# A one-column gelu behind each block's last output tile, and the mask of one attention unit moved to TensorE

## The chip, the cores and the metric

The kernel runs on one core of a Trainium2 chip. Times are microseconds (us) on the device. The time before is 360.91 us, the median of three runs (360.09 to 361.98); the profiled execution took 361.28 us, and its span, the part that the trace covers, is 359.4 us.

## What is computed

Two things in a row: windowed attention over 8 batches with 8 heads each, then a gated feed-forward block on the result. Cut to what matters:

```python
# attention: q, k, v are (8, 8, 576, 64) float32
rel = pos[:, None] - pos[None, :]
mask_plain = (rel >= 0) & (rel < 32)                        # heads 0 to 3
mask_dil   = (rel >= 0) & (rel < 128) & (rel % 4 == 0)      # heads 4 to 7
scores = where(mask, q @ k.T / 8, -1e9)
x = softmax(scores) @ v              # put together to (4608, 512)

# feed-forward: w_gate and w_val are (512, 1536), w_out is (1536, 512)
g = x @ w_gate
out = (gelu(g) * (x @ w_val)) @ w_out
```

## The kernel before

**Units and blocks.** Two heads of one batch make a unit: 32 units, four for each batch, two "plain" and two "dilated". The 4608 tokens are cut into 9 blocks of 512. A block `c` is first multiplied with the gate and value weights (`ffn1`, 12 steps `nb`), then with the output weights (`ffn2`, four tiles `tb` of 128 tokens, 12 matmuls each). The attention of later units is woven into that work. Its schedule is written by hand: the order of the program text is the order of the instructions on each engine.

```python
def geglu(nb, banks):
    g = ffn.tile([P, CH], F16, tag="g")                     # a pool of three
    nc.scalar.activation(g, ps[:, banks[0], :], AF.Gelu)                          # L584, ACT
    nc.vector.scalar_tensor_tensor(u_all[:, nb, :], g, USCALE,
                                   ps[:, banks[1], :], ALU.mult, ALU.mult)        # L585, DVE
```

Each step of `ffn1` fills one PSUM bank with gate sums (weights `wg`) and one with value sums (`wv`), four matmuls each on line 562. There are two pairs of banks, so step `nb` writes into the banks of step `nb - 2`: the gate bank is free once ScalarE's gelu has read it, the value bank once VectorE's multiplication has.

Where the block before it ended with attention work that the new block still waits for (a flag `late`: blocks 2, 3 and 4), the first two steps are interleaved: all matmuls of steps 0 and 1 that have their inputs come first, the rest follow, and only then come the two `geglu`:

```python
def ffn1_two(c, pairs, order, split):
    kcs = parts_of(order)
    for group in [kcs[:-1], kcs[-1:]] if split else [[kc] for kc in kcs]:
        for nb in range(2):
            for gi in range(2):
                ffn1_part(c, nb, gi, pairs[nb][gi], group)
    for nb in range(2):
        geglu(nb, pairs[nb])
```

The output tile is read out of PSUM by ScalarE and stored:

```python
def store(c, tb, bank, eng):
    osb = osbp.tile([P, DM], F32, tag="osb")
    if eng == "act":
        nc.scalar.activation(osb, ps[:, bank, :], AF.Copy, bias=0.0, scale=1.0 / USCALE)   # L602
```

**Scores of a unit.** `emit_s` computes the scores on TensorE, takes the exponential on ScalarE, and masks in one of two ways. Either VectorE multiplies the exponentials with a mask of zeros and ones, or (`pe_mask`) TensorE first writes a bias of 0 or -60000 into the four banks, by a matmul with the identity, and adds the scores to it:

```python
def emit_s(n, b0, pe_mask=False):
    ...
    else:                                                   # a dilated unit; DW is 288
        if pe_mask:
            for i in range(4):
                mm(ps[:, b0 + i, 0:DW], ident, bias_d, start=True, stop=False, ...)   # L359
        ...                                                 # 12 small matmuls, L373
        pt = prb.tile([P, 4, DW], F16, tag="P", name=f"P{n}")
        nc.scalar.activation(pt, ps[:, b0 : b0 + 4, 0:DW], AF.Exp, bias=0.0, scale=scale)  # L375
    if pe_mask:
        return None
    def emit_mask():
        nc.vector.tensor_tensor(pt, pt, mb, ALU.mult)                                 # L383
    return emit_mask
```

**Values of a unit.** `emit_pv` multiplies the masked exponentials with ones and with the values (L455); VectorE then divides, in four steps: a transpose of the sums (L513), a reciprocal (L520), a transpose back (L522) and the product into `xT` (L537 for a dilated unit).

**The main loop.** A table says at which output tile and before which of its 12 matmuls each piece of attention is done: `v` the values of a unit and its reciprocals, `s` the scores of the next, `x` the product of the division, `m` the mask, `w` a unit's values with a division in two parts. The numbers are tile and matmul; 12 means after the tile's store.

```python
scores   = {0: range(4, 8), 1: range(8, 12), 2: range(12, 17), ...}
values_b = {1: range(8, 12), 2: range(12, 16), 3: range(17, 20), 4: range(22, 24), 5: range(27, 28)}
biased = (6, 7)
places = {
    1: "0.0m 1.3v 1.3s 1.3x 1.3m 2.5v 2.5s 2.5x 2.5m 3.0s 3.0m 3.6v 3.6x 3.12w",
    ...
}
for c in range(NCH):
    ...                              # ffn1, 12 steps of gelu; one emit_s behind them
        lone = c in values_b         # true for blocks 1 to 5
        for tb in range(4):
            ...
            ffn2(c, tb, bank, hooks)
            store(c, tb, bank, "dve" if c > 5 and tb == 3 else "act")
            ...
        late = lone and len(values_b[c]) > 2
```

In block 1 the scores of unit 8 come behind the last gelu, and those of unit 9 before matmul 3 of tile 1, behind the values of unit 8. Unit 9 is the second unit of batch 2, and it is a dilated one.

Of the kernel before, what the change touches and what calls it, by code (L numbers as in the profile page):

```python
# [9 lines left out]
F16 = mybir.dt.float16  # L10
F32 = mybir.dt.float32
AF = mybir.ActivationFunctionType
# [26 lines left out]
def kernel(  # L39
# [10 lines left out]
    nc = tc.nc  # L50
# [3 lines left out]
    P = 128  # L54
# [3 lines left out]
    CH = 512  # L58
# [25 lines left out]
    ffn = ctx.enter_context(tc.tile_pool(name="ffn", bufs=3))  # L84
    osbp = ctx.enter_context(tc.tile_pool(name="osbp", bufs=4))

    ones = const.tile([P, CH], F16, tag="ones")
# [135 lines left out]
    def load_batch_plain(b):  # L223
        st = load_qk_plain(b)
        sv = new_v(b)
        v_plain(b, sv, nc.sync)
        return st, sv
# [5 lines left out]
    def load_batch_rest(b):  # L233
        st, sv = tiles["plain", b]
        qd, rd = load_qk_dil(b)
        qp = cast_qk_plain(b, st)
        load_v_dil(b)
        v_cast(b, sv)
        new_qt(b)
        qtp_, qtd_, _ = tiles["qT", b]  # L240
        dst = qtd_.rearrange("p t h m i -> p (t h m) i")
        nc.sync.dma_start_transpose(out=dst[:, :, 0:P], in_=qd.rearrange("p t h r d -> p (t h r d)"))
        nc.sync.dma_start_transpose(out=dst[:, :, P:NCL], in_=rd.rearrange("p t h r d -> p (t h r d)"))
        dst = qtp_.rearrange("p t h c -> p (t h) c")
        for kb in range(5):
            n = min(P, S - kb * P)
            nc.sync.dma_start_transpose(
                out=dst[:, :, kb * P : kb * P + n], in_=qp[0:n, kb].rearrange("p t h d -> p (t h d)")
            )
        last_keys(b, 0, HK, nc.gpsimd)  # L250
# [6 lines left out]
    def is_plain(n):  # L257
        return pair(n) < NHP // 2
# [221 lines left out]
    def norm_both_r(n, b0):  # L480
        dt = nrm.tile([P, 18, 32], F32, tag="dt", bufs=1)
        for hl in range(2):
            nc.vector.transpose(  # L483
                dt[64 * hl : 64 * hl + 64].rearrange("p b c -> p (b c)"), both_rows(1 - hl, b0, hl)
            )
        recip(n, dt)
# [80 lines left out]
    def ffn1(c, nb, banks):  # L567
        for gi in range(2):
            ffn1_part(c, nb, gi, banks[gi], parts_of(range(NKC)))
        geglu(nb, banks)  # L570
# [12 lines that stand above are left out]
        g = ffn.tile([P, CH], F16, tag="g")  # L583
        nc.scalar.activation(g, ps[:, banks[0], :], AF.Gelu)  # L584
        nc.vector.scalar_tensor_tensor(u_all[:, nb, :], g, USCALE, ps[:, banks[1], :], ALU.mult, ALU.mult)  # L585

    def ffn2(c, tb, bank, hooks=None):
        for fc in range(NNB):
            for hook in (hooks or {}).get(fc, ()):
                hook()  # L590
            nc.tensor.matmul(  # L591
                ps[:, bank, :],
                u_all[:, fc, tb * P : (tb + 1) * P],
                wo_t[fc // 4][:, fc % 4, :],
                start=(fc == 0),
                stop=(fc == NNB - 1),
            )
# [57 lines left out]
    def den(n, b0, wide=False):  # L655
        emit_pv(n, b0, ("den",), wide)
        norm_r(n, b0, wide)
# [49 lines left out]
    scores = {0: range(4, 8), 1: range(8, 12), 2: range(12, 17), 3: range(17, 22), 4: range(22, 27), 5: range(27, 32)}  # L707
    values_b = {1: range(8, 12), 2: range(12, 16), 3: range(17, 20), 4: range(22, 24), 5: range(27, 28)}
    values_a = {3: {4: 16}, 4: {2: 20, 6: 21}, 5: {1: 24, 4: 25, 7: 26}, 6: {1: 28, 4: 29, 7: 30, 10: 31}}
    biased = (6, 7)  # L710

# [10 lines left out]
    for c in range(NCH):  # L724
        if 1 <= c and c + 2 < B:
            tiles["plain", c + 2] = load_batch_plain(c + 2)
            load_batch_rest(c + 2)
        pv_at = values_a.get(c, {})
        s_list = list(scores.get(c, ()))
        if c < 2:  # L730
            pairs = ((2, 3), (0, 1))
        else:
            pairs = (ends, (mm0 + 1, mm0 + 2))
        SB = 4 - mm0

        masks = []
        pend = None
        for nb in range(NNB):
            if nb == 0 and c < 2:
                ffn1_two(c, ((4, 5), (6, 7)) if c == 0 else ((6, 7), (0, 1)), range(NKC), False)  # L740
            elif nb == 0 and late:
                ffn1_two(c, pairs, (2, 3, 0, 1) if c in (2, 3) else range(NKC), True)
            elif nb > 1 or not (c < 2 or late):
                ffn1(c, nb, pairs[nb % 2])
            if pend is not None:
                (norm_both_x if is_plain(pend) else norm_x)(pend, SB)
                pend = None
            if nb in pv_at:
                pend = pv_at[nb]
                if is_plain(pend):  # L750
                    emit_both(pend, SB)
                    norm_both_r(pend, SB)
                else:
                    emit_pv(pend, SB, wide=True)
                    norm_r(pend, SB, wide=True)
            if c == 0 and nb in (9, 10):
                t_plain(1, q61, nb - 9, 4 + 2 * (nb - 9), ("act", "dve"))
            if c == 0 and nb in (8, 11):
                rr = rd1.rearrange("p t h r d -> p t (h r d)")
                hp = nb // 11  # L760
                t_dil(1, hp, qd1, 4096 + 512 * hp, 5120 + 512 * hp, ("dve", "dve"))
                t_rest(1, hp, (rr[:, 0], rr[:, 1]), 6144 + P * hp)
            if nb == NNB - 1 and c > 0 and s_list:
                n = s_list.pop(0)
                masks.append(emit_s(n, SB, pe_mask=n in biased))

        def s_next():
            if s_list:
                n = s_list.pop(0)
                masks.append(emit_s(n, SB, pe_mask=n in biased))  # L770

        def mask_next():
            mask = masks.pop(0) if masks else None
            if mask is not None:
                mask()


        def md(n):
            mask_next()
            den(n, 0, wide=True)  # L780

        if c == 0:
            load_batch_rest(2)
            ffn2(c, 0, 0, {5: [s_next]})
            store(c, 0, 0, "act")
            ffn2(c, 1, 1, {4: [s_next], 8: [lambda: md(4)]})
            store(c, 1, 1, "act")
            s_next()
            ffn2(c, 2, 0, {4: [lambda: md(5)], 6: [s_next], 9: [lambda: md(6)]})
            store(c, 2, 0, "act")  # L790
            ffn2(c, 3, 1, {2: [lambda: md(7), lambda: num(4, 4)], 8: [lambda: num(5, 6)]})
            store(c, 3, 1, "act")
            num(6, 2)
            num(7, 4)
        else:
            todo = list(values_b.get(c, ()))
            lone = c in values_b

            ends = (3, 0) if c == 1 else ends
            going = []  # L800

            def do(kind, tb):
                if kind == "s":
                    s_next()
                elif kind == "m":
                    mask_next()
                elif kind == "x":
                    norm_x(*going.pop(0))
                elif kind == "v":
                    n, flip = todo.pop(0), ends[tb % 2] != mm0  # L810
                    bank = mm0 + 1 - flip
                    emit_pv(n, bank, flip=flip)
                    norm_r(n, bank, flip=flip)
                    going.append((n, bank, flip))
                else:
                    n = todo.pop(0)
                    emit_pv(n, SB)
                    norm_parts(n, SB, min(S, (c + 2) * CH - n // NHP * S))

            for tb in range(4):  # L820
                at = [(fc, kind) for t, fc, kind in places.get(c, ()) if t == tb]
                hooks = {}
                for fc, kind in at:
                    if fc < NNB:
                        hooks.setdefault(fc, []).append(lambda kind=kind, tb=tb: do(kind, tb))
                bank = ends[tb % 2] if lone else mm0 + tb
                ffn2(c, tb, bank, hooks)
                store(c, tb, bank, "dve" if c > 5 and tb == 3 else "act")
                for fc, kind in at:
                    if fc == NNB:  # L830
                        do(kind, tb)

            late = lone and len(values_b[c]) > 2
            if c == 3:
                mm0 = 4 - mm0
            if c == 3 or not lone:
                ends = (mm0, mm0 + 3)
            while masks:
                mask_next()
# [28 lines left out]
```

The softmax here doesn't subtract the row's maximum and nothing guards it: scores larger than these inputs give would overflow.

## Time and profile before

| | busy, us | share of the span |
|---|---|---|
| PE (TensorE matmul) | 338.7 | 94% |
| DVE (VectorE) | 204.4 | 57% |
| ACT (ScalarE) | 145.8 | 41% |
| POOL (GpSimd) | 78.4 | 22% |

How to read it: L584 is line 584 of the kernel before; "PEld" is TensorE's load of weights, which goes on beside its matmuls. In the timeline a row gives the start, the time from the start of its first to the end of its last instruction, the engine, the line, what is written and read, and how many there are; brackets tell how long the engine had been idle and what ended that. The busy time of matmuls overlaps in part, since they are pipelined: rows of 512-column matmuls start 0.216 us apart (four of them take 0.86 us from the first's start to the next group's), although one is listed with 0.38 us.

The table load is a row of its own, ACT_TABLE_LOAD, with 1283 ns each: 7 on line 584 (gelu), 4 on line 375 and 2 on line 353 (exponential), and one at the start of the program.

### The profile page before, as it was taken

What the parts mean: (1) busy time and instruction counts of PE and PEld (TensorE: products, weight loads), DVE (VectorE), ACT (ScalarE), POOL (GpSimd) and SP (SyncE); (2) the same over time, 40 slices, a digit from 0 to 9 for tenths busy, and PEclk for the clock granted to TensorE, in tenths of its full rate; (3) what the DMA queues carried; (4) which work ended last, traced back from release to release, by engine and by line L of the source; (5) the groups of instructions that cost most, each with busy time, mean ns of one, the idle gap of its engine ahead of it and who ended that gap; (6) DMA issues with size and microseconds to landing.
All of it is one profiled execution on the core that took longest, in us unless ns stands there. A gap on an engine that the chain in (4) does not pass through costs nothing.

```text
span 359.4 us, 5962 instructions
## 1 busy us (share of the span) xinstructions
PE 338.7 (94%) x2326; PEld 164.2 (46%) x2326; DVE 204.4 (57%) x314; ACT 145.8 (41%) x212; POOL 78.4 (22%) x110
## 2 busy tenths in 40 slices
PE   5889999999898999899989999999999999999995
PEld 2554454444443444344544444544454444444442
DVE  3595446744695448773768855894489514403320
ACT  1733255253444354435453357326633123313320
POOL 2580334630531350063004500140000000000000
PEclk9889999999999999999999999999999999999999
DMA  8999999999999997699149952793100020020002
GB/s 198 237 181 211 221 154 204 166 154 255 199 124 213 186 163 152 161 174 142 60 120 193 135 95 79 179 158 79 69 22 0 31 88 0 3 84 32 2 30 88
DMA packets 107292, 45.31 MB, mean 126 GB/s; under 512 B 83040, under 2 KB 102496, under 8 KB 107264
## 3 DMA queue, kind: packets, MB, share of 16 engines
q1 hardware_dynamic: 84272, 31.21, 39.8%
q0 software_dynamic: 21456, 12.01, 26.6%
q10 hardware_dynamic: 1536, 1.70, 2.1%
q8 instruction: 18, 0.29, 0.3%
q14 instruction: 10, 0.08, 0.1%
HBM read 40.13 MB, written 9.44 MB: 138 GB/s over the span
## 4 chain that ended last, share of the span: by engine, by line
PE 66%; DVE 13%; DMA 13%; issue 3%; POOL 2%; ACT 1%; ACTq 0%; SPq 0%; DVEq 0%; POOLq 0%
PE ps L562 40%; PE ps L591 20%; PE ps L455 4%; DMA xT<-in_k_dram 4%; DMA st<-in_k_dram 3%; DMA wv<-in_moe_w_val_dram 3%; DMA wo<-in_moe_w_out_dram 2%; DVE P L383 2%; DVE xT L537 2%; DVE rb L522 2%; DVE dt L513 2%; DVE dt L483 2%; DVE u_all L585 2%; DVE xT L493 1%; DMA sv<-in_v_dram 1%
## 5 line engine op out<-in xcount | busy, mean ns | idle before, releaser
L562 PE MATMUL ps<-xT,wg 128*128 128x512 f16 x432 | 114.0, 379 | 5.1 <-ACT g L584 4.1
L585 DVE SCALAR_TENSOR_TENSOR u_all<-g,ps 128x512 f16<-128x512 f16 x108 | 72.8, 684 | 80.1 <-PE ps L562 70.0
L562 PE MATMUL ps<-xT,wv 128*128 128x512 f16 x432 | 113.8, 379 | 0.3 <-ACT osb L602 0.3
L584 ACT ACTIVATE g<-ps 128x512 f16<-128x512 f32 x108 | 63.7, 597 | 116.8 <-PE ps L562 116.6
L591 PE MATMUL ps<-wo,u_all 128*128 128x512 f16 x432 | 100.3, 380 | 0.1
L562 PEld LDWEIGHTS <-wv 128*128 128x128 f16 x432 | 42.2, 98 | 52.7 <-issue 2.6
L562 PEld LDWEIGHTS <-wg 128*128 128x128 f16 x432 | 41.1, 98 | 52.5 <-issue 5.5
L591 PEld LDWEIGHTS <-u_all 128*128 128x128 f16 x432 | 39.4, 98 | 45.4 <-issue 0.6
L602 ACT ACTIVATE osb<-ps 128x512 f32<-128x512 f32 x33 | 19.7, 598 | 38.1 <-PE ps L591 36.6
L199 POOL CAST qp<-st 128x2048 f16<-128x2048 f32 x6 | 11.4, 1896 | 100.1 <-DMA sv<-in_v_dram 54.3
L513 DVE STREAM_TRANSPOSE dt<-ps 128x576 f32<-128x576 f32 x23 | 17.9, 780 | 14.5 <-PE ps L455 14.3
L522 DVE STREAM_TRANSPOSE rb<-rc 128x576 f32<-128x576 f32 (+4 forms) x34 | 25.3, 743 | 1.2
L375 ACT ACTIVATE P<-ps 128x1152 f16<-128x1152 f32 x16 | 18.1, 1131 | 16.9 <-PE ps L373 13.0
L353 ACT ACTIVATE P<-ps 128x960 f16<-128x960 f32 x16 | 15.5, 970 | 12.8 <-PE ps L343 12.8
L537 DVE TENSOR_TENSOR xT<-ps,rb 128x576 f16<-128x576 f32 x16 | 17.9, 1129 | 0.3
L604 DVE TENSOR_SCALAR osb<-ps 128x512 f32<-128x512 f32 x3 | 2.1, 692 | 27.8 <-PE ps L591 27.8
L455 PE MATMUL ps<-P,ones 128*64 128x96 f16 (+5 forms) x174 | 12.0, 253 | 5.0 <-DVE P L383 2.9
L383 DVE TENSOR_TENSOR P<-P,mask_d 128x1152 f16<-128x1152 f16 x12 | 9.6, 800 | 10.2 <-ACT P L375 10.2
L383 DVE TENSOR_TENSOR P<-P,mask_p 128x1344 f16<-128x1344 f16 x14 | 12.4, 891 | 5.0 <-ACT P L354 4.9
L455 PEld LDWEIGHTS <-ones 128*64 128x64 f16 x174 | 7.7, 112 | 14.9 <-issue 10.8
L584 ACT ACT_TABLE_LOAD x7 | 9.0, 1283 | 12.4 <-PE ps L562 12.3
L483 DVE STREAM_TRANSPOSE dt<-ps 64x576 f32<-64x576 f32 x14 | 10.9, 781 | 0.4
(81 smaller groups left out, 238.9 us busy)
## 6 DMA issues: line engine op xcount, KB each, us to landing
out_dram<-osb SPq DMA_DIRECT2D x36, 256.0 KB, 2.0
sv<-in_v_dram SPq DMA_DIRECT2D x40, 128.0 KB, 3.6
st<-in_q_dram SPq DMA_DIRECT2D x24, 128.0 KB, 3.6
st<-in_k_dram SPq DMA_DIRECT2D x24, 128.0 KB, 3.1
qd<-in_q_dram POOLq DMA_DIRECT2D x7, 256.0 KB, 5.3
qd<-in_k_dram POOLq DMA_DIRECT2D x7, 256.0 KB, 6.7
vd<-in_v_dram POOLq DMA_DIRECT2D x7, 256.0 KB, 6.8
wg<-in_moe_w_gate_dram POOLq DMA_DIRECT2D x3, 512.0 KB, 7.5
```

Of the source, the lines that this page charges most:

```text
L375: nc.scalar.activation(pt, ps[:, b0 : b0 + 4, 0:DW], AF.Exp, bias=0.0, scale=scale)
L383: nc.vector.tensor_tensor(pt, pt, mb, ALU.mult)
L455: nc.tensor.matmul(o, lhs, rhs, start=st, stop=True, skip_group_check=True)
L483: nc.vector.transpose(dt[64 * hl : 64 * hl + 64].rearrange("p b c -> p (b c)"), both_rows(1 - hl, b0, hl))
L513: nc.vector.transpose(dst, den)
L522: nc.vector.transpose(rb[:, 0 : 32 * nb].rearrange("p (b c) -> p b c", c=32), bass.AP(tensor=rc.tensor, offset=rc.offset, ap=[rc.ap[0], [1 ...
L537: nc.vector.tensor_tensor(dst.rearrange("p (i m s) -> p i m s", m=2, s=2), num, rb.rearrange("p (s m i) -> p i m s", s=2, m=2), ALU.mult,)
L562: nc.tensor.matmul(ps[:, bank, :], w[:, kc, ns], xT[kc][:, tok], start=first, stop=end)
L584: nc.scalar.activation(g, ps[:, banks[0], :], AF.Gelu)
L585: nc.vector.scalar_tensor_tensor(u_all[:, nb, :], g, USCALE, ps[:, banks[1], :], ALU.mult, ALU.mult)
L591: nc.tensor.matmul(ps[:, bank, :], u_all[:, fc, tb * P : (tb + 1) * P], wo_t[fc // 4][:, fc % 4, :], start=(fc == 0), stop=(fc == NNB - 1),)
L602: nc.scalar.activation(osb, ps[:, bank, :], AF.Copy, bias=0.0, scale=1.0 / USCALE)
```

## The change

Two things change, and they have nothing to do with each other.

First, a new function issues a gelu of one column, whose result nobody reads, behind the last output tile of each of the blocks 1 to 5. ScalarE holds the table for one set of functions at a time, and gelu and the exponential are in different sets; the compiler puts a table load ahead of the first activation that needs another set. The one-column gelu is meant to draw the load forward, to a place where ScalarE has nothing to do.

Second, unit 9 joins the list of units whose mask is applied by TensorE as a bias instead of by VectorE.

```diff
@@ -584,6 +584,11 @@
         nc.scalar.activation(g, ps[:, banks[0], :], AF.Gelu)
         nc.vector.scalar_tensor_tensor(u_all[:, nb, :], g, USCALE, ps[:, banks[1], :], ALU.mult, ALU.mult)
 
+    def gelu_table():
+
+        g = ffn.tile([P, CH], F16, tag="g")
+        nc.scalar.activation(g[:, 0:1], ones[:, 0:1], AF.Gelu)
+
@@ -707,7 +712,7 @@
-    biased = (6, 7)
+    biased = (6, 7, 9)
@@ -829,6 +834,8 @@
                 for fc, kind in at:
                     if fc == NNB:
                         do(kind, tb)
+            if lone:
+                gelu_table()
 
             late = lone and len(values_b[c]) > 2
```

The order of instructions on each engine, compiled from both kernels, differs in nothing else: ScalarE has five more rows (the one-column gelus; the number of table loads stays), TensorE four more matmuls of 288 columns with their weight loads, VectorE one multiplication less.

## The prediction

> **What bounds the kernel now.** I read the shares of the engines first, then the list of who waited for whom for TensorE, then the timeline round each place where that list points, and last the chain of work that ended last.
>
> ```profile
> PE 338.7 (94%) x2326; PEld 164.2 (46%) x2326; DVE 204.4 (57%) x314; ACT 145.8 (41%) x212; POOL 78.4 (22%) x110
> ```
>
> TensorE is the bound, with 359.4 - 338.7 = 20.7 us idle. Whatever is to be won by a change that gives TensorE no less work must come out of that. The waits of TensorE name two causes that the change touches:
>
> ```profile
> PE ps L562 <- ACT g L584: 4.1, 3, 1.4
> PE ps L455 <- DVE P L383: 2.9, 6, 0.9
> ```
>
> TensorE waited three times, 4.1 us in all, for a gelu (L584), and six times, 2.9 us in all, for a mask on VectorE (L383). The first wait is always between two blocks. This is the timeline where block 1 ends and block 2 begins:
>
> ```profile
> 105.33 0.60 ACT L602 ACTIVATE osb<-ps 128x512 f32<-128x512 f32 x1 [2.38 <-PE ps L591]
> ...
> 109.35 1.28 ACT L584 ACT_TABLE_LOAD   x1 [3.42 <-PE ps L562]
> 109.54 0.38 PE L562 MATMUL ps<-xT,wv 128*128 128x512 f16 x1
> ...
> 109.60 0.36 DVE L554 TENSOR_TENSOR xT<-ps,rb 128x192 f16<-128x192 f32 x1
> 110.64 1.08 ACT L584 ACTIVATE g<-ps 128x512 f16<-128x512 f32 x2
> 111.27 1.28 DVE L585 SCALAR_TENSOR_TENSOR u_all<-g,ps 128x512 f16<-128x512 f16 x2 [1.32 <-ACT g L584]
> 111.29 1.02 PE L562 MATMUL ps<-xT,wg 128*128 128x512 f16 x4 [1.38 <-ACT g L584]
> ```
>
> ScalarE is idle for 3.42 us after its last output tile and starts the table load only when the matmuls of step 0 are done: the load stands under the wait of the gelu behind it. TensorE ends step 1 at 109.92 and needs the gate bank of step 0 for step 2, so it stands for 1.38 us until the gelu has read that bank. The same load of 1.28 us is ahead of a wait at the start of block 3 (TensorE again at 150.38) and block 4 (188.53). The start of block 3 has something that the others lack:
>
> ```profile
> 148.44 1.28 ACT L584 ACT_TABLE_LOAD   x1 [3.34 <-PE ps L562]
> 148.51 0.42 DVE L554 TENSOR_TENSOR xT<-ps,rb 128x256 f16<-128x256 f32 x1
> 148.62 0.38 PE L562 MATMUL ps<-xT,wv 128*128 128x512 f16 x1
> 148.85 0.85 DVE L383 TENSOR_TENSOR P<-P,mask_p 128x1344 f16<-128x1344 f16 x1
> 149.73 1.08 ACT L584 ACTIVATE g<-ps 128x512 f16<-128x512 f32 x2
> 150.36 1.28 DVE L585 SCALAR_TENSOR_TENSOR u_all<-g,ps 128x512 f16<-128x512 f16 x2 [0.66 <-ACT g L584]
> ```
>
> VectorE is busy with a mask until 149.70, most of the time that ScalarE loads its table. It goes on with the product of step 0 after only 0.66 us of idleness. For the mask of unit 9 the timeline of block 1 shows:
>
> ```profile
> 95.95 1.15 DVE L537 TENSOR_TENSOR xT<-ps,rb 128x576 f16<-128x576 f32 x1
> 96.36 0.60 ACT L602 ACTIVATE osb<-ps 128x512 f32<-128x512 f32 x1 [0.91 <-DMA sv<-in_v_dram]
> 97.01 1.29 DVE L383 TENSOR_TENSOR P<-P,mask_d 128x1152 f16<-128x1152 f16 x1
> 98.35 0.44 PE L455 MATMUL ps<-P,ones 128*64 128x192 f16 x8 [0.95 <-DVE P L383]
> ...
> 99.20 0.78 DVE L513 STREAM_TRANSPOSE dt<-ps 128x576 f32<-128x576 f32 x1 [0.91 <-PE ps L455]
> ```
>
> The exponentials of unit 9 were ready long before, but VectorE had the division of unit 8 to do first; TensorE waits 0.95 us. From there the chain of work that ended last runs through VectorE to the end of the block: L513, L520, L522, L537, the mask of unit 10 (L383), TensorE at 103.11, and the same again to 106.73. So what moves at 98.35 moves the rest of the block.
>
> **What the Trainium skill says.** "ScalarE: Activation LUTs", section "What ACT_TABLE_LOAD costs", puts a load at about 1283 ns and adds a drain of about 1380 ns. The trace agrees with the first: 1283 ns for all seven loads on L584. It shows nothing of the second here: the gelu starts 1.29 us after its load does (109.35 to 110.64). I count 1.28 us for a load, not 2.66. The same section puts an activation with immediate operands at 186 ns + 0.833 ns a column: 613 ns for 512 columns, where the trace has 597. Taking the page's slope off the trace's value, a one-column gelu takes an estimated 0.17 us. "PSUM — Partial Sum Buffer", section "PSUM bank collisions raise a hardware error", says that two engines may not touch one bank at once, so accesses are guarded bank by bank. That fits the wait of TensorE for the gelu: a gate bank comes free with the gelu, a value bank only with VectorE's product.
>
> **The change part by part.**
>
> *The loads (blocks 1 to 5).* Their number stays at 13 for gelu and the exponential together; five of them move, each behind the last output tile, with a one-column gelu behind it. In the compiled order the moved load carries no wait on TensorE.
>
> - Block 1 to 2: the output tile ends at 105.93, so load and one-column gelu end near 105.93 + 1.28 + 0.17 = 107.4, two microseconds before they are needed. The gelu of step 0 starts at 109.35 instead of 110.64 and ends at 109.95; TensorE goes on at about 110.0 instead of 111.29. VectorE is free at 109.96 and does its product from 109.97 to 110.66; TensorE wants that value bank after four gate matmuls, at 110.0 + 0.86 = 110.86. No new wait. Gain 1.29 us.
> - Block 2 to 3: the gelu ends at 149.04, TensorE goes on at 149.09 and wants the value bank at 149.95. VectorE comes to the product only after its mask, at 149.72, and ends it at about 150.40. TensorE starts there at 150.43, where it started at 151.24 before. Gain 151.24 - 150.43 = 0.81 us; the other 0.48 us go into a wait for VectorE.
> - Block 3 to 4: gelu from 186.59, TensorE on at 187.24 instead of 188.53. VectorE ended its mask at 185.66 and waited 2.85 us. Gain 1.29 us.
> - Block 4 to 5: here the load stood directly behind the output tile already (223.15, no idle time), and TensorE didn't wait for the gelu. The one-column gelu delays the first gelu by 0.1 to 0.2 us (estimate), but VectorE's second product was waiting for TensorE. Gain 0.
> - Block 5 to 6: the load waited only 0.31 us (259.82). It moves forward by that, and the one-column gelu takes half of it back. VectorE's second product there starts at 262.44, when TensorE's value matmuls of step 1 end by their own pace. I count 0.
>
> Sum: 1.29 + 0.81 + 1.29 = 3.39 us.
>
> *The mask of unit 9.* VectorE loses 1.29 us of work. TensorE gets four matmuls of 288 columns. Those of unit 6 took from 57.66 to 58.25, where the scores followed: 0.59 us, and those of unit 7 took 0.58 us. With them, the scores of unit 9 end and the output matmuls start at 94.21 + 0.58 = 94.79; 14 matmuls of 0.216 us and 0.1 us for the change to small matmuls (as between 105.13 and 105.23) lead to 97.91. The exponential of unit 9, from 94.32 + 0.58, is done at 96.03; the division of unit 8 frees its banks at 97.10; the output tile at 96.36 + 0.58 + 0.60 = 97.54. All are ahead of 97.91. So the values of unit 9 start at 97.91 instead of 98.35: gain 0.44 us. VectorE is free then, so its chain to the end of the block starts 0.44 us earlier, and TensorE follows it.
>
> Together 3.39 + 0.44 = 3.83 us of 360.91: 357.1 us. The profile's span should go from 359.4 to about 355.6.
>
> **The rivals.**
>
> 1. *The wait only changes its name.* TensorE would stand for VectorE's product where it stood for the gelu. This is so in part at block 3, where the mask is in the way. If it held at all three places, no more than 0.8 us each would be left: 360.91 - 2.4 - 0.4 = 358.1. Against it: the 1.32 and 2.85 us that VectorE itself waited for the gelu at blocks 2 and 4.
> 2. *The bias costs TensorE what the mask cost.* TensorE is the fullest engine, and 0.58 of the 0.95 us go back as work. Were the value matmuls held by something else that the trace doesn't separate from the mask, such as the bank of the output tile, the gain would be nothing or a loss of up to 0.58: 357.5 to 358.1. The division of unit 8, which ends at 97.10, speaks against it.
> 3. *Transfers take over.* Work 3.8 us earlier could run into loads that don't move. Against it: the last transfer in the chain ends at 53.19, and the keys that block 2 needs at 128.7 are complete at 106.6. For it: VectorE's and GpSimd's work shifts against each other, and the mask of unit 9 took 1.29 us where others of its shape take 0.76. It might cost a few tenths.
> 4. *The load is drawn forward further than meant, or a drain comes back.* If the one-column gelu cost a whole drain (the page's 1.38 us), it would still end at 108.8 in block 1 to 2, ahead of 109.35; at blocks 5 and 6 the gelu would come up to 1.4 us later, and 1 to 2 us of the gain would be lost: about 358.6.
>
> **Range and chances.** The three waits are seen in the trace, all on TensorE, and their lengths are known to 0.1 us, so the sum is uncertain by perhaps half a microsecond, mostly downward by rivals 1, 2 and 4. The runs before spread over 1.9 us. I take 355.8 to 358.7. Faster by 2% would mean under 353.7, more than the two waits that the change touches hold together (4.1 + 0.95 us); slower by 2% would take a wait that nothing points to. Chances: faster by over 2% 0.02, within 2% 0.97, slower 0.01.
>
> **What would show it right or wrong.** Right: no wait of TensorE for a gelu at the starts of blocks 2, 3 and 4; one of about 0.5 us for VectorE's product at block 3; the table loads at 105.5 or so with the gelu two microseconds behind; TensorE's wait before the values of unit 9 gone; busy time of TensorE up by half a microsecond, idle time down by over four. Wrong: if a moved load still waits for TensorE, if the gelu of step 0 starts over 0.1 us after its matmuls, or if VectorE is the new releaser at blocks 2 and 4.

## The result, and the profile after

The changed kernel takes 357.50 us, the median of four runs (357.14 to 357.76); the kernel before takes 360.98 us, with one more run than above (360.09 to 361.98). The ratio is 0.990, its 95% interval 0.987 to 0.993. That is 3.5 us less, where 3.83 had been forecast.

In the kernel after, lines behind 589 have moved by five: L590 is the one-column gelu, L596 the output matmul and L607 the output tile on ScalarE. The shares of the engines, from the page after:

```profile
PE 340.1 (96%) x2330; PEld 165.3 (47%) x2330; DVE 202.5 (57%) x313; ACT 146.6 (41%) x217; POOL 78.2 (22%) x110
```

TensorE's idle time went from 20.7 to 355.3 - 340.1 = 15.2 us, more than the span fell, because its busy time went up by 1.4 us where half a microsecond had been forecast. The kernel with the gelus alone (e1 below) gives TensorE no added work, and its busy time is 340.9, so these sums don't show what the bias costs. These are its waits, three lines out of the list of waits after:

```profile
PE ps L455 <- DVE P L383: 2.1, 5, 0.6
...
PE ps L562 <- DVE u_all L585: 0.2, 1, 0.2
...
PE ps L562 <- DVE xT L534: 0.2, 1, 0.2
```

The wait for a gelu, 4.1 us before, is gone from the list. A new one of 0.2 us is for VectorE's product (L585). The wait for masks lost its longest, the 0.9 us of unit 9. This is the end of block 1 and the start of block 2, from the timeline after:

```profile
104.60 0.60 ACT L607 ACTIVATE osb<-ps 128x512 f32<-128x512 f32 x1 [2.37 <-PE ps L596]
...
105.21 1.28 ACT L590 ACT_TABLE_LOAD   x1
...
106.51 0.21 ACT L590 ACTIVATE g<-ones 128x1 f16<-128x1 f16 x1
...
108.63 1.08 ACT L584 ACTIVATE g<-ps 128x512 f16<-128x512 f32 x2 [1.91 <-PE ps L562]
...
109.26 1.28 DVE L585 SCALAR_TENSOR_TENSOR u_all<-g,ps 128x512 f16<-128x512 f16 x2
109.28 1.02 PE L562 MATMUL ps<-xT,wg 128*128 128x512 f16 x4
```

The load follows the output tile at once, and ScalarE then waits 1.91 us with the table in place. The gelu starts with its matmuls' end, and the row of TensorE has no bracket: it didn't stand. At the start of block 3 the mask is in the way, as it was:

```profile
146.85 0.85 DVE L383 TENSOR_TENSOR P<-P,mask_p 128x1344 f16<-128x1344 f16 x1
147.10 1.02 PE L562 MATMUL ps<-xT,wg 128*128 128x512 f16 x4
147.62 1.28 DVE L585 SCALAR_TENSOR_TENSOR u_all<-g,ps 128x512 f16<-128x512 f16 x2
...
148.35 1.02 PE L562 MATMUL ps<-xT,wv 128*128 128x512 f16 x4 [0.23 <-DVE u_all L585]
```

The value matmuls come 1.25 us after the gate matmuls instead of 0.86. And the mask of unit 9:

```profile
92.89 0.44 PE L455 MATMUL ps<-P,ones 128*64 128x192 f16 x8
...
93.53 0.66 PE L359 MATMUL ps<-bias_d,ident 128*128 128x288 f16 x4
...
94.13 0.29 PE L373 MATMUL ps<-qTd 64*128 64x128 f16 x4
...
97.62 0.44 PE L455 MATMUL ps<-P,ones 128*64 128x192 f16 x8
```

The bias takes 94.13 - 93.53 = 0.60 us, and the values of unit 9 start without a wait.

To compare traces I take distances between landmarks on TensorE, since the opening, until the first values of unit 8, differs by more than the effects do (91.59 to 93.35 us in the traces of kernels with no change there). V8 and V9 are the starts of the values of units 8 and 9, G2, G3 and G4 those of the gate matmuls of step 2 in blocks 2, 3 and 4, W3 those of the value matmuls of step 2 in block 3. The rows of V8, W3 and G4 before, and of G4 after, which stand nowhere else here:

```profile
93.19 0.44 PE L455 MATMUL ps<-P,ones 128*64 128x192 f16 x8
...
151.24 1.03 PE L562 MATMUL ps<-xT,wv 128*128 128x512 f16 x4
...
188.53 1.02 PE L562 MATMUL ps<-xT,wg 128*128 128x512 f16 x4 [1.38 <-ACT g L584]
```

```profile
184.37 1.02 PE L562 MATMUL ps<-xT,wg 128*128 128x512 f16 x4
```

| distance, us | before | after | won | forecast |
|---|---|---|---|---|
| V8 to V9 | 98.35 - 93.19 = 5.16 | 97.62 - 92.89 = 4.73 | 0.43 | 0.44 |
| V9 to G2 | 111.29 - 98.35 = 12.94 | 109.28 - 97.62 = 11.66 | 1.28 | 1.29 |
| G2 to W3 | 151.24 - 111.29 = 39.95 | 148.35 - 109.28 = 39.07 | 0.88 | 0.81 |
| W3 to G4 | 188.53 - 151.24 = 37.29 | 184.37 - 148.35 = 36.02 | 1.27 | 1.29 |
| G4 to the end of the span | 359.4 - 188.53 = 170.87 | 355.3 - 184.37 = 170.93 | -0.06 | 0 |

Spans are given to a tenth, so the last row is zero within their rounding. Together 3.80 us. The span fell by 4.1 us; the other 0.30 us are an earlier V8 (93.19 to 92.89), in a part of the program that the change doesn't touch.

### The profile page after: what moved, and what is told of

Same layout as the page of the kernel before. It is cut to its first block, busy times and chain, and to the rows that moved or that the text cites. A ratio compares the mean times of both kernels' runs of the same rounds, so it can differ in the third digit from the quotient of the medians.

```text
span 355.3 us, 5974 instructions
## 1 busy us (share of the span) xinstructions
PE 340.1 (96%) x2330; PEld 165.3 (47%) x2330; DVE 202.5 (57%) x313; ACT 146.6 (41%) x217; POOL 78.2 (22%) x110
## 4 chain that ended last, share of the span: by engine, by line
PE 78%; DVE 13%; DMA 3%; issue 3%; ACT 2%; ACTq 0%; DVEq 0%
PE ps L562 46%; PE ps L596 22%; PE ps L455 5%; DMA xT<-in_k_dram 3%; DVE rb L522 2%; DVE dt L513 2%; DVE dt L483 2%; DVE u_all L585 2%; DVE xT L537 2%; DVE P L383 1%; PE ps L373 1%; DVE xT L493 1%; PE ps L343 1%; DVE rc L520 1%; PE ps L359 1%
## 5 line engine op out<-in xcount | busy, mean ns | idle before, releaser
L585 DVE SCALAR_TENSOR_TENSOR u_all<-g,ps 128x512 f16<-128x512 f16 x108 | 72.7, 683 | 76.8 <-PE ps L562 68.4
L596 PE MATMUL ps<-wo,u_all 128*128 128x512 f16 x432 | 100.2, 380 | 0.0
L596 PEld LDWEIGHTS <-u_all 128*128 128x128 f16 x432 | 39.4, 98 | 45.2 <-issue 0.2
L607 ACT ACTIVATE osb<-ps 128x512 f32<-128x512 f32 x33 | 19.7, 598 | 38.1 <-PE ps L596 37.5
L383 DVE TENSOR_TENSOR P<-P,mask_d 128x1152 f16<-128x1152 f16 x11 | 8.3, 757 | 10.2 <-ACT P L375 10.2
L183 POOL CAST vp<-sv 128x1024 f16<-128x1024 f32 x8 | 8.5, 1059 | 12.0 <-DMA sv<-in_v_dram 12.0
```

Source lines behind the costliest of these rows:

```text
L596: nc.tensor.matmul(ps[:, bank, :], u_all[:, fc, tb * P : (tb + 1) * P], wo_t[fc // 4][:, fc % 4, :], start=(fc == 0), stop=(fc == NNB - 1),)
```

## The experiments

My theory: a load under a gelu's wait costs TensorE its 1.28 us at three places, up to what VectorE takes back; a mask on VectorE is a second and smaller matter; the parts add. The rivals: one part did it all; the bias costs what the mask did; loads anywhere are worth something; a load has a hidden drain.

**e1_tables_only.** The gelus without the bias.

```diff
-    biased = (6, 7, 9)
+    biased = (6, 7)
```

> The kernel after with unit 9 masked by VectorE again, so that only the one-column gelus are left. Theory (the two parts are independent and add): 3.4 us faster than the kernel before (1.3 us at block 2, 0.8 to 0.9 at block 3, 1.3 at block 4), about 357.5; TensorE's wait of 0.95 us before the values of unit 9 is back. Rival (most of the gain came from the mask and its train of work on VectorE): under 2 us faster.

Measured: 357.47 us, ratio 0.990 (0.987 to 0.993). V9 to G2 11.64 us, G2 to W3 39.08, W3 to G4 36.01: 3.45 us won at the three places. The theory holds, the rival falls. But the time is that of the whole change, so the bias's 0.43 us are not to be seen in it. And V8 to V9 is 5.33 us, longer than before:

```profile
96.48 1.45 DVE L383 TENSOR_TENSOR P<-P,mask_d 128x1152 f16<-128x1152 f16 x1
...
96.77 1.24 POOL L218 DMA_DIRECT2D vr<-in_v_dram  x2
```

The mask of unit 9 took 1.45 us here and ended at 97.93, 0.08 us ahead of the end of GpSimd's issue of transfers (L218) at 98.01.

**e2_bias_only.** The bias without the gelus.

```diff
-    biased = (6, 7)
+    biased = (6, 7, 9)
```

> The kernel before with unit 9 biased on TensorE and no one-column gelu. Theory: 0.44 us faster than before (the values of unit 9 start 0.44 us earlier with respect to those of unit 8), about 360.5; the three waits for a gelu of 1.38 us are all there. Rival (the four bias matmuls cost TensorE what the mask cost): no gain, or up to 0.6 us slower.

Measured: 361.00 us, ratio 1.000 (0.998 to 1.002). In its trace V8 to V9 is 4.74 us and V9 to G2 12.92: 0.42 us won against the trace before, and the waits for the gelu untouched. The interval is 0.6 us wide on each side, so the time doesn't tell 0.44 from nothing; the rival's loss of 0.6 is at its edge.

**e3_unit9_unmasked.** Kernel before, unit 9's mask left out.

```diff
-        if pe_mask:
+        if pe_mask or n == 9:
             return None
```

> The kernel before with no mask at all for unit 9: its mask is left out, so that its keys outside the window count too. Theory (TensorE waited for VectorE's mask and for nothing else): the values of unit 9 start when TensorE comes to them, about 1.0 us earlier than before; 1.0 us faster, 359.9. With the bias this was 0.44 us, so the difference of about 0.58 us is what the four matmuls cost. Rival (a bank wait stands behind the mask's): the gain stays at about 0.4 us, as with the bias.

Measured: 360.08 us, ratio 0.997 (0.996 to 0.998), which is 0.6 to 1.3 us faster. V8 to V9 is 96.80 - 92.66 = 4.14 us, 1.02 less than before, and TensorE doesn't wait there. So no bank wait stands behind the mask's, and the bias costs 4.74 - 4.14 = 0.60 us of what leaving out the mask would give.

**e4_tables_45.** Kernel before with the one-column gelu only behind blocks 4 and 5.

```diff
-            if lone:
+            if c in (4, 5):
                 gelu_table()
```

> The kernel before with the one-column gelu behind blocks 4 and 5 only. Theory: no change, within 0.1 us, since TensorE didn't wait for a table load at the starts of blocks 5 and 6; the gelu starts 0.1 us later at block 5 and at the same time at block 6. Rival (every load drawn forward is worth a part of its 1.28 us): up to 1 us faster; rival (a one-column gelu costs a drain too): 1 to 2 us slower.

Measured: 360.98 us, ratio 1.000 (0.999 to 1.002). From G4 to the end 358.9 - 188.04 = 170.86 us, as before (170.87). Both rivals fall: a load that TensorE doesn't wait for is worth nothing, and a one-column gelu is no drain. The trace had a surprise in the part that is the same as before. V8 to V9 was 4.63 us instead of 5.16, though VectorE masks unit 9:

```profile
97.03 0.75 DVE L383 TENSOR_TENSOR P<-P,mask_d 128x1152 f16<-128x1152 f16 x1
...
97.35 1.25 POOL L218 DMA_DIRECT2D vr<-in_v_dram  x2
...
97.83 0.44 PE L455 MATMUL ps<-P,ones 128*64 128x192 f16 x8 [0.41 <-DVE P L383]
```

The mask took 0.75 us, and TensorE waited 0.41. That is even 0.1 us less than with the bias. So what the bias wins or loses depends on whether that execution's mask is held up: 1.29 and 1.45 us before and in e1, 0.75 here.

**e5_three_loads.** Kernel after with two more loads behind blocks 1 to 3.

```diff
             if lone:
                 gelu_table()
+            if c in (1, 2, 3):
+                exp_table()            # the same, with AF.Exp
+                gelu_table()
```

> The kernel after, and behind blocks 1, 2 and 3 also a one-column exponential and a second one-column gelu, so that three loads stand there in place of one. Theory (a load costs 1.28 us and nothing more, and is hidden up to ScalarE's spare time there, which after the change is 2.0 us at block 2, 2.0 at block 3 and 0.9 at block 4): the further work is 3.0 us, so the first gelu comes 1.0, 1.1 and 2.2 us later than in the kernel after; TensorE loses 1.0 and 2.2 us at blocks 2 and 4 and 0.7 at block 3, where 0.4 us went to a mask anyway: 3.9 us slower than after, about 361.3. Rival (a load has a drain of 1.4 us too that overlaps with idle time so far): about 2.8 us more at each block, 12 us slower. Rival (loads aren't on TensorE's path): as after.

Measured: V9 to G4 is 188.47 - 97.85 = 90.62 us against 184.37 - 97.62 = 86.75 after: 3.87 us more, for 3.9 expected. The timeline of ScalarE at block 4 shows what one load costs (L595 is the one-column exponential):

```profile
183.40 1.28 ACT L590 ACT_TABLE_LOAD   x1
184.69 0.21 ACT L590 ACTIVATE g<-ones 128x1 f16<-128x1 f16 x1
184.92 1.28 ACT L595 ACT_TABLE_LOAD   x1
186.21 0.20 ACT L595 ACTIVATE g<-ones 128x1 f16<-128x1 f16 x1
186.43 1.28 ACT L590 ACT_TABLE_LOAD   x1
187.73 0.21 ACT L590 ACTIVATE g<-ones 128x1 f16<-128x1 f16 x1
187.84 1.06 ACT L584 ACTIVATE g<-ps 128x512 f16<-128x512 f32 x2
```

From load to load 1.51 to 1.52 us, the one-column activation included. The drain of 1.38 us that rival 4 reckons with is not in it. The time was 362.36 us, ratio 1.004 (1.002 to 1.005), about 1 us above what I expected; its runs spread from 359.8 to 363.5, and the trace (span 359.4) doesn't show that microsecond.

**e6_mask_late.** Kernel after, mask of unit 16 behind the first two products of block 3.

```diff
-        2: "... 3.7s 3.12w 3.12m",
+        2: "... 3.7s 3.12w",
@@ the loop of ffn1, block 3, ahead of step 1's other work
+            if nb == 1 and c == 3:
+                for mask in held:      # left over from block 2
+                    if mask is not None:
+                        mask()
@@ the end of a block
-            while masks:
+            held = masks if c == 2 else []
+            while masks and c != 2:
                 mask_next()
```

> The kernel after with the mask of unit 16, which stands at the end of block 2, moved behind VectorE's first two products of block 3. Theory (the 0.4 us that TensorE lost at block 3 between the gate and the value matmuls of step 2 are this mask): the value matmuls start 0.86 us after the gate matmuls instead of 1.25; 0.4 us faster than after, 357.1. Rival (VectorE's product is late for another reason): no change.

Measured: the value matmuls start 148.24 - 147.38 = 0.86 us after the gate matmuls, and V9 to G4 is 0.39 us less than after (184.25 - 97.89 = 86.36). The mask was the reason. 356.95 us, ratio 0.989 (0.987 to 0.991). The times of this and of the next two kernels don't stand clear of the kernel after (0.990, 0.987 to 0.993); what they win is read from the distances.

**e7_block0.** Kernel after with a one-column gelu behind block 0 too.

```diff
             store(c, 3, 1, "act")
+            gelu_table()
             num(6, 2)
```

> The kernel after with one more one-column gelu behind the last output tile of block 0. There the load waited for TensorE too (71.42 in the profile before), but the third pair of banks was free, so that TensorE stood for the gelu for 0.3 us only (73.54 to 73.85). Theory: 0.3 us faster than after, 357.2. Rival (every load that waits for TensorE costs its 1.28 us): 1.3 us faster.

Measured: value matmuls of step 2 to gate matmuls of step 3 in block 1: 74.08 - 73.21 = 0.87 us, where it was 73.85 - 72.68 = 1.17 before. Won 0.30 us, and not 1.28, as it should be if the third pair of banks stands in for the gelu. 357.37 us, ratio 0.990 (0.988 to 0.992).

**e8_mask_first.** The gelus, no bias, and unit 9's mask ahead of unit 8's last product.

```diff
-    biased = (6, 7, 9)
+    biased = (6, 7)
-        1: "0.0m 1.3v 1.3s 1.3x 1.3m 2.5v ...",
+        1: "0.0m 1.3v 1.3s 1.3m 1.3x 2.5v ...",
```

> The one-column gelus, no bias for unit 9, and VectorE does the mask of unit 9 ahead of the product that ends the division of unit 8 instead of behind it. Theory (what TensorE waits for is the last of these two on VectorE): the mask no longer ends last, but the division does, 1.2 us later than now, at 97.9 in the times of the profile before; the values of unit 9 start their first matmuls without waiting and the rest at 97.9, and the time is that of the kernel after within 0.1 us. Rival (the mask alone counts, the banks are free): 0.5 us faster than after. Rival (the order counts for nothing, as VectorE has the same work): 0.4 us slower than after.

Measured: 357.12 us, ratio 0.989 (0.987 to 0.991). The mask took 0.72 us and the division ended at 97.77. The transpose of unit 9's sums started 98.58 - 93.35 = 5.23 us after V8, where it was 99.20 - 93.19 = 6.01 before and 98.48 - 92.89 = 5.59 after. So this order wins 0.36 us on the kernel after without any work on TensorE; I had expected the same time within 0.1 us. I had counted a mask as long as the one before, and this one was not held up.

**e9_gpsimd_quiet.** The gelus, no bias, and GpSimd's work for batch 3 in another order.

```diff
         qd, rd = load_qk_dil(b)
+        if b == 3:
+            load_v_dil(b)
         qp = cast_qk_plain(b, st)
-        load_v_dil(b)
-        v_cast(b, sv)
+        if b != 3:
+            load_v_dil(b)
+            v_cast(b, sv)
         ...
         last_keys(b, 0, HK, nc.gpsimd)
+        if b == 3:
+            v_cast(b, sv)
```

> The one-column gelus, no bias for unit 9, and for batch 3 GpSimd issues its transfers of v before its casts of q and k and casts v at the end, so that GpSimd has nothing to do while VectorE masks unit 9. Theory (the long mask of unit 9, 1.29 us in the profile before and 1.45 us with the gelus alone, is the mask held until GpSimd has issued the transfers of line 218; where the two missed each other it took 0.75): the mask takes 0.75 to 0.80 us and the values of unit 9 start 4.6 us after those of unit 8, where they started 5.2 to 5.3 us after, and 4.7 with the bias; so the bias has nothing left to win, and the time is that of the kernel after within 0.1 us. Rival (the mask is long for another reason, such as the transfers themselves): 1.3 to 1.5 us again.

Measured: with GpSimd idle the mask took 0.76 us, and V8 to V9 was 98.13 - 93.51 = 4.62 us, with TensorE's wait at 0.41. That is the theory's number. The time isn't: 358.49 us, ratio 0.994 (0.991 to 0.996), runs from 357.3 to 359.6. The trace, of a run of 357.61 us, doesn't show the loss: V8 to G4 is 184.87 - 93.51 = 91.36 us, where it is 91.48 after. But the new order set GpSimd's casts beside another mask, that of unit 12, which took 0.76 us before and 1.25 here:

```profile
129.01 1.07 POOL L183 CAST vp<-sv 128x1024 f16<-128x1024 f32 x1
129.45 1.25 DVE L388 TENSOR_TENSOR P<-P,mask_d 128x1152 f16<-128x1152 f16 x1 [1.45 <-ACT P L380]
```

In this kernel and in e10 to e12, L388 is the mask, L348 the scores of a plain unit and L567 the gate and value matmuls.

**e10_together.** e6, e7, e8 and e9 in one kernel (their diffs together, without the bias).

> The version that the runs so far point to: the one-column gelus behind blocks 0 to 5, no bias for unit 9 but its mask ahead of the division of unit 8, the mask of unit 16 behind the first two products of block 3, and GpSimd quiet during the mask of unit 9. From the parts as the traces showed them (0.3 us at block 1, 0.4 for the order on VectorE, 0.4 at block 3): 1.1 us faster than the kernel after, 356.4. Rival (the parts lie behind one another's waits): no more than the largest of them, 0.4 us.

Measured: V8 to G4 183.66 - 92.83 = 90.83 us against 184.37 - 92.89 = 91.48 after, 0.65 us less, and block 0's 0.3 us besides; 1.1 had been expected. The transpose of unit 9's sums starts 98.05 - 92.83 = 5.22 us after V8, and 98.98 - 93.51 = 5.47 in e9: with GpSimd idle beside both masks, the order alone is worth 0.25 us. In the time nothing of it appears: 357.62 us, ratio 0.992 (0.989 to 0.995), runs from 356.2 to 359.5.

**e11_all_masks_first.** As e10, with every mask ahead of the division beside it.

```diff
-        2: "0.0m 1.3v 1.3s 1.3x 1.3m 2.5v 2.5s 2.5x 2.5m ...
+        2: "0.0m 1.3v 1.3s 1.3m 1.3x 2.5v 2.5s 2.5m 2.5x ...      # blocks 1 and 3 likewise, 4 with 2.4, 5 at 1.3 alone
```

> As the last one, with the mask ahead of the division wherever the two stand together (blocks 1 to 4). Theory (the division frees the banks 1.2 us later, so that only the first matmuls of the next unit start earlier): 0.1 us at each of four places, 0.4 us faster than the last one at most. Rival (a later division holds up the next unit's values): slower by some tenths.

Measured: 355.34 us, ratio 0.986 (0.983 to 0.989), the fastest of all; five of its six runs lie between 354.2 and 355.9. That is 2.3 us below e10 where 0.4 had been expected, and it isn't explained: the profiled execution was its slowest, 358.76 us. It shows something else instead:

```profile
139.81 0.44 PE L348 MATMUL ps<-qTp 64*128 64x160 f16 x8
141.95 0.20 PE L348 MATMUL ps<-qTp 64*128 64x64 f16 x2 [1.70 <-DMA qTp<-qp]
...
144.85 1.46 PE L567 MATMUL ps<-xT,wg 128*128 128x512 f16 x3
```

TensorE stood 1.70 us for the transposes of batch 4, and soon after it ran slower (three matmuls in 1.46 us, where 0.81 is usual). The granted clock says why: 0.50 for 3.41 us, from 143.46 to 146.87, and 1.00 on either side. The wait and half of the slow stretch are about 3.4 us (an estimate), most of what sets this run apart from the other five. With GpSimd's new order that batch comes in later: its first transpose starts at 123.74 here, against 122.66 before and 122.75 after. That is not the whole cause, since it starts at 125.50 in e10, where TensorE doesn't wait; but one of the transposes took 7.2 us to land here, and none over 5.0 in e10. Whether the same wait spreads the runs of e9 and e10 isn't shown, as their profiled executions don't have it.

**e12_together_bias.** As e10, with the bias in place of the mask ahead of the division.

> As e10, but with the bias for unit 9 in place of its mask ahead of the division. Theory (the bias costs TensorE 0.58 us, the mask without GpSimd beside it costs a wait of 0.4 us or less): the transpose of the sums of unit 9 starts 5.6 us after the values of unit 8 begin, where it is 5.2 in e10; 0.35 us slower than e10, 356.8. Rival (the bias is worth its 0.44 us): 0.4 us faster than e10.

Measured: V8 to G4 183.72 - 92.39 = 91.33 us, 0.50 us more than e10, for 0.35 expected. Up to G2 it is 16.38 against 16.02 us, 0.36 more; the rest falls in block 2, where the mask of unit 13 took 1.01 us beside GpSimd. In the time, 357.22 us, ratio 0.990 (0.988 to 0.992), the two aren't told apart.

## Why the prediction was right

- *A load costs 1.28 us and hangs under the gelu's wait.* Right. e1 won 3.45 us with the loads alone, e4 nothing where TensorE didn't wait, and e5 lost what it should by the spare time (3.87 us for 3.9).
- *The one-column gelu takes 0.17 us.* It takes 0.20 to 0.21 us, but the next activation starts 0.11 us after it (220.28 to 220.39 at block 5), so it costs less than forecast.
- *At block 3 the mask takes back 0.48 us.* Right, the size was off by 0.07 (1.29 - 0.88 = 0.41 us went into it): the product started at 147.62, 0.08 us ahead of the mask's end in the trace. The bracket of that row has only 0.23 us, where about 0.5 had been named as a sign; the distance of 1.25 us instead of 0.86 has 0.39. e6 took the mask away and the rest was there.
- *Blocks 5 and 6 win nothing.* Right (e4, and the last row of the table).
- *The bias costs 0.58 us and wins 0.44 us.* In this pair of traces right to 0.01, and the bias's own cost was 0.60. That it met so closely was luck: "0.95 us of waiting" was one execution's value. The mask took 1.29 and 1.45 us in the two traces where it was stuck beside GpSimd's issue and 0.75 us in e4, where V8 to V9 was 4.63 us. There the bias would lose 0.1 us. I named the 1.29 us under rival 3 and didn't draw that conclusion. What the bias is worth over many executions stays open: e2 says 0.0 us, give or take 0.6, and the gelus alone (e1, 357.47 us) were as fast as the whole change (357.50). The 3.5 us measured are accounted for by the loads.
- *The rivals.* Rival 1 held at block 3 alone. Rival 2 fell by e3. Rival 3 had no part in the change itself, and came up when GpSimd's order was changed (e11). Rival 4 fell by e5.

Masks and GpSimd's casts hold each other up, and that much the fourteen traces show. Of their 357 masks on VectorE, the 328 with nothing of GpSimd's beside them took 0.71 to 0.88 us. Of the other 29, fifteen took longer, 0.92 to 1.68 us. Thirteen of these began while a cast or copy of GpSimd was running, and ended 0.60 to 0.71 us after it, as if they had only begun there. In turn a cast (L187) that started during a mask took 0.97 to 1.06 us, where it takes 0.40 to 0.47 elsewhere.

The Trainium skill, "SBUF — State Buffer", section "SBUF: two separate sides", states that a VectorE instruction with two inputs in SBUF and a GpSimd instruction that reads SBUF share a pair of ports, and the one that starts first has it for its whole length, while the other is blocked. For casts and copies the traces agree, with the figures above. Why unit 9's mask was held before and in e1, the other two of the fifteen, stays open. It had only issues of transfers beside it, of which the section doesn't say that they read SBUF. It ended 0.08 us ahead of the end of L218, and with GpSimd idle (e9) the mask took 0.76 us; but in e4 and e8 masks ran beside the same issues, and neither was longer than usual. The masks that started up to 0.43 us after the issue of line 213 went through (e4, e8), those at 0.47 and 0.62 us were held (e1 and before). Four points make no rule.

## What to carry to other kernels

Look for a table load whose idle time before it ends with the wait of the activation behind it: it can be drawn forward by an activation of one column that depends on nothing, and it wins what the engine behind it really waits, no more (here 1.28 us, 0.88, 0.30 or nothing). Before work moves from VectorE to TensorE to end a wait, try the order on the engine that is waited for, which gives TensorE no work (here worth 0.25 us with GpSimd idle, seen in the distances and not in the times). And take a wait of which GpSimd is a part from several traces, not from one.

## What the runs showed of the hardware

A load followed by a one-column activation repeats every 1.5 us (e5), so a switch of tables on an otherwise idle ScalarE is 1.28 us and no more. The same mask on the same data took 0.72 to 1.45 us, depending on what GpSimd did beside it; thirteen masks that began during a cast or copy of GpSimd took 0.92 to 1.68 us and ended 0.60 to 0.71 us after it. In e11 TensorE's granted clock fell to 0.50 for 3.41 us, 1.5 us after a wait of 1.70 us had ended; in e5 a wait of 2.29 us at the start of block 4 was followed by the usual pace, four matmuls in 0.86 us, at a clock of 1.00. So a wait may cost more than its own length, but the length alone doesn't decide it.
